# Chunk attention and SoLU feed-forward on one core: one copy for the turned probabilities of tiles 0 to 5, v loaded by halves of heads

## The chip, the cores and the metric

The kernel runs on one core of a Trainium2 chip. The metric is the device time of one execution in microseconds (us), taken as the median of several runs. Engines are named as in the profile: PE (TensorE matmul), PEld (its weight loads), DVE (VectorE), ACT (ScalarE), POOL (GpSimd) and SP (SyncE, which here only issues transfers; SPq is its queue).

## The reference

Attention inside chunks of 64 tokens, then a feed-forward layer on the joined heads:

```
B, H, S, D = 8, 8, 576, 64                  # 9 chunks of 64 tokens per batch
scores = q_c @ k_c^T / sqrt(D)               # within each chunk
attn   = softmax(scores)
x      = (attn @ v_c), heads joined          # 4608 tokens x 512
h      = x @ w_in                            # 512 -> 1024
e      = exp(h - max(h));  sm = e / sum(e)
solu   = h * sm
ln     = (solu - mean) / sqrt(var + 1e-6) * g_ln
out    = ln @ w_out                          # 1024 -> 512
```

## The kernel before

The 4608 tokens are cut into 36 tiles of 128 tokens, each of two chunks (c = 0, 1) of 64. The eight heads are taken as four pairs (hp), with j = 0, 1 inside a pair. Matrix products of the feed-forward layer are made of three products of rounded parts (`wi_l`, `wi_h`, `wo_l`, `wo_h` are the low and high parts of the weights).

The program has two parts. The first tiles and the preparation of the weights are an order written out by hand, the string START: each word is a step with its arguments, and the words are run one after the other; each engine does its instructions in the order in which they were issued. The words that matter here: `P:x` loads a raw unit of weights (0 to 3 for w_in, 4 to 7 for w_out), `n:i` loads q and k of tile i in their natural layout into the tile `nat` (two slots, used in turn), `v:i` loads v of tile i (`load_v`), `N:i:x` turns q or k on PE, `S:i` makes the scores (`scores`), `A:i` and `B:i` the softmax, `T:i` turns the probabilities of tiles 0 to 5 on PE and copies them out (`attn_transpose`), `V:i` makes the product with v (`values`, then `x_high` on ACT and `x_low` on DVE), `b`, `c`, `C`, `t`, `d` prepare a unit of weights (w_b, w_a, their join, high part, low part), `M:i` is the first feed-forward product, `w` is a matmul without a use that fills time. `K` and the loop behind START do the rest of the tiles, with PE as the engine that the order is built around.

Every transfer of START goes out on SP's queue, one behind the other. The framework gives the transfers eight landing counters (DMAHW0 to DMAHW7) in turn, so each one's issue waits until the transfer eight places before it has landed.

Probabilities. `scores` puts tile i's scores into `sx`, with the chunk's 64 query tokens on partitions c * 64 and the pair member j choosing one of two banks. Softmax gives `s_e`, 128 tokens x 8 heads x 64 keys. `attn_transpose` turns it with four PE transposes into a bank `tp`, so that partition j * 64 + key and column hp, query token hold a probability. The product with v needs, on chunk c's 64 partitions of `attn_t` (AT), the keys of chunk c for all heads, since v's tokens of chunk c lie on those partitions. So four ACT copies (c by j) take 64 partitions each, half of them from one half of the partitions to the other. Tiles from 6 on are turned by DVE and moved by transfers instead (`attn_turn`).

Of the kernel before, what the change touches and what calls it, by code (L numbers as in the profile page):

```python
# [65 lines left out]
def chunk_attention_then_solu_ffn(  # L66
# [15 lines left out]
    CH = 64  # L82
    NCH = S // CH
    HP = H // 2
# [7 lines left out]

    MS = nc.gpsimd
    PE_TURNED = 6
    PH2 = (1,)
    ORD = 5

# [12 lines left out]
    def po():  # L110
# [10 lines left out]
    pe, dve, act, pool, sync = (  # L121
        order.engine(e)
        for e in (nc.tensor, nc.vector, nc.scalar, nc.gpsimd, nc.sync)
    )
# [3 lines left out]
    def queue_of(word):  # L128
        return {"pool": pool, "act": act}.get(moved.get(word), sync)
# [7 lines left out]
    def bank():  # L137
        return ps_t.tile([P, FF // 2], F32, name="tp")
# [120 lines left out]
    QT, KT, V, QS, KS = {}, {}, {}, {}, {}  # L259
# [17 lines left out]
    AT = const.tile([P, 2, 2, H, 32], F32, name="attn_t")  # L277
# [23 lines left out]
    def chunk_of(i, c):  # L301
        n = 2 * i + c
        return n // NCH, n % NCH
# [19 lines left out]
    def tile_parts(i):  # L323

        (b0, n0), (b1, n1) = chunk_of(i, 0), chunk_of(i, 1)
        if b0 == b1:
            return [(0, P, b0, n0 * CH)]
        return [(0, CH, b0, n0 * CH), (CH, P, b1, n1 * CH)]
# [9 lines left out]

    def load_v(i):
        V[i] = work.tile([P, H, D], F32, name="v_sb", bufs=4)  # L340
        for p0, p1, b, s in tile_parts(i):
            arriving[i // 2].insert(0, queue_of(f"v:{i}").dma_start(
                V[i][p0:p1], v[b, :, s:s + p1 - p0, :].rearrange("h t d -> t h d")
            ))
# [19 lines left out]
    sx = ps_a.tile([P, 2, 2, HP, CH], F32, name="sx")  # L364
    sy = None

    def attn(i):
        return sy if order.on and i % 2 else sx

    def scores(i):  # L370
        sx = attn(i)
        for hp in range(HP):
            for c in range(2):
                for j in range(2):
                    rows, cols = slice(j * D, (j + 1) * D), slice(c * CH, (c + 1) * CH)
                    pe.matmul(
                        sx[cols, j, 0, hp],
                        QT[i][rows, hp, cols],
                        KT[i][rows, hp, cols],
                        start=True,  # L380
                        stop=True,
                    )
# [24 lines left out]
    def softmax_b(i):  # L407
# [6 lines left out]
        yield  # L414
        a = st[i, "e"] = work.tile([P, H, CH], F32, name="s_e") if i < PE_TURNED else e
        (pool if f"B:{i}" in moved else dve).tensor_tensor(
# [3 lines left out]
    def attn_transpose(i):  # L420

        a = st.pop((i, "e"))
        pt = bank().rearrange("p (a t) -> p a t", t=P)
        for hp in range(HP):
            pe.transpose(
                pt[:, hp, :],
                a[:, 2 * hp:2 * hp + 2, :].rearrange("p j k -> p (j k)"),
                ident,
            )
        yield  # L430
        for c in range(2):
            cols = slice(c * CH, (c + 1) * CH)
            to = AT[cols, :, i % 2].rearrange("p g (h j) t -> p j h g t", j=2)
            for j in range(2):
                act.copy(
                    to[:, j],
                    pt[j * CH:(j + 1) * CH, :, cols].rearrange(
                        "p h (g t) -> p h g t", t=32
                    ),
                )  # L440

    def attn_turn(i):
        a = st.pop((i, "e"))
# [17 lines left out]
    def values(i):  # L463
        sx = attn(i)
        for hp in range(HP):
            for j in range(2):
                for c in range(2):
                    rows = slice(c * CH, (c + 1) * CH)
                    pe.matmul(
                        sx[j * D:(j + 1) * D, c, 1, hp],  # L470
                        V[i][rows, 2 * hp + j, :],
                        AT[rows, :, i % 2, 2 * hp + j, :],
                        start=True,
                        stop=True,
                    )

    def start_values(i):
        values(i)
        yield
        x_high(i)  # L480
        yield
        x_low(i)
# [19 lines left out]
    def ffn_in(i):  # L502
        xh, xl = st[i, "x"]
        pool_h = ps_h2 if i in PH2 else ps_h
        ph = st[i, "h"] = pool_h.tile([P, 2, HALF], F32, name="ph")
# [254 lines left out]
    def warm(n):  # L760
# [9 lines left out]
    todo = {  # L770
        "P": load_pair, "n": load_natural,
        "v": load_v, "g": load_g, "Q": load_batch, "q": load_some,
        "G": scale_g, "N": turn_natural, "S": scores, "A": start_softmax, "B": softmax_b,
        "T": attn_transpose, "U": attn_turn, "V": start_values, "c": unit_scale,
        "b": unit_bits, "C": unit_join, "t": unit_high, "d": unit_low, "M": ffn_in, "X": solu_a, "Y": solu_b,
        "R": variance, "Z": z_turn, "z": z_half, "F": product, "o": store, "O": store_one,
# [18 lines left out]
    for i in range(first, NT):  # L795
# [7 lines left out]
        if i + 3 < NT:  # L803
            load_v(i + 3)
# [12 lines left out]
        if odd:  # L817
            for m in (i + 1, i + 2):
                if m + 2 < NT:
                    scores(m + 2)  # L820
                if m < NT:
                    values(m)
# [78 lines left out]
```

## Time and profile before

| | |
|---|---|
| median of 3 runs | 473.31 us (472.98 to 473.34) |
| the profiled execution | 471.33 us, of it 469.5 us span |
| PE busy | 461.0 us (98%) |
| PEld, DVE, ACT, POOL busy | 381.4, 368.4, 260.7, 149.3 us |
| granted clock of PE | 0.999 of full speed |
| DMA busy, first 24.37 us / rest | 0.99 / 0.66 |

The span runs from the first to the last instruction. An engine's busy share is an average over the whole span; where an engine is always busy, what counts is when it gets its first work and what makes it wait.

### The profile page before, as it was taken

The page shows a single profiled execution, that of the slowest core. Times are in us where ns is not written, and L with a number is a line of the kernel's source. Part 1 is how long each engine was busy: PE and PEld are TensorE (multiplying, and loading weights), DVE is VectorE, ACT ScalarE, POOL GpSimd, SP SyncE. Part 2 cuts the span into 40 slices and gives each one's busy share as a digit, 9 for nine tenths or more (in the row PEclk, how much of TensorE's full clock was granted, in tenths as well). Part 3 has the DMA queues.
Part 4 walks back from the last instruction along what each step waited for, and adds up shares of the span by engine and source line. Part 5 has one row for each costly group of instructions (what it writes and reads, how often), then busy time and mean ns, then how long its engine had stood idle before and what let it go on. Part 6 is the DMA issues. An engine that isn't in the chain of part 4 may idle for free.

```text
span 469.5 us, 11066 instructions
## 1 busy us (share of the span) xinstructions
PE 461.0 (98%) x4210; PEld 381.4 (81%) x4210; DVE 368.4 (78%) x516; ACT 260.7 (56%) x425; POOL 149.3 (32%) x300
## 2 busy tenths in 40 slices
PE   8799999999999999999999999999999999999997
PEld 6588887888888888888888888888888888888886
DVE  1999997988779887878788878787979797954441
ACT  4889985554544555454646464545545454545451
POOL 1116536150505151505050505042505141424430
PEclk9999999999999999999999999999999999999999
DMA  9999989778886788786267696858644434343221
GB/s 253 305 285 244 194 145 179 163 194 144 200 147 173 136 202 143 186 153 178 52 162 142 162 163 171 160 138 170 157 108 111 114 99 128 87 116 100 72 77 66
DMA packets 192924, 72.57 MB, mean 155 GB/s; under 512 B 177188, under 2 KB 177960, under 8 KB 191976
## 3 DMA queue, kind: packets, MB, share of 16 engines
q1 hardware_dynamic: 186200, 58.89, 56.1%
q0 software_dynamic: 6528, 12.86, 10.4%
q8 instruction: 33, 0.54, 0.5%
q14 instruction: 19, 0.16, 0.1%
q10 hardware_dynamic: 144, 0.13, 0.1%
HBM read 36.70 MB, written 9.44 MB: 98 GB/s over the span
## 4 chain that ended last, share of the span: by engine, by line
PE 93%; DMA 2%; ACT 2%; SPq 2%; DVE 1%; issue 0%; DVEq 0%; ACTq 0%
PE po L57 42%; PE ph L57 41%; PE tp L57 6%; PE sx L57 5%; DMA w_raw<-in_moe_w_in_dram 2%; SPq L57 2%; DVE z_b L57 1%; ACT attn_t L57 0%; ACT wi_h L57 0%; ACT z L57 0%; ACT w_a L57 0%; ACT z_h L57 0%; ACT w_b L57 0%; ACT o_sb L57 0%; ACT kT L57 0%
## 5 line engine op out<-in xcount | busy, mean ns | idle before, releaser
L57 ACT ACTIVATE z<-ph,h_nmax 128x1024 f32<-128x1024 f32 x36 | 40.2, 1116 | 131.7 <-DVE h_nmax L57 131.6
L57 PE MATMUL po<-wo_l,z_h 128*128 128x512 f32 (+1 forms) x288 | 113.1, 393 | 0.0
L57 PE MATMUL ph<-wi_l,x_h 128*128 128x512 f32 x288 | 112.9, 392 | 0.0
L57 PE MATMUL ph<-wi_h,x_h 128*128 128x512 f32 x288 | 112.1, 389 | 0.0
L57 PE MATMUL po<-wo_h,z_l 128*128 128x512 f32 (+1 forms) x288 | 111.6, 387 | 0.0
L57 PE MATMUL po<-wo_h,z_h 128*128 128x512 f32 (+1 forms) x288 | 111.5, 387 | 0.0
L57 POOL DMA_DIRECT2D z_t<-z_b x144 | 71.8, 506 | 23.7 <-DVE z_b L57 19.7
L57 PE MATMUL ph<-wi_h,x_l 128*128 128x512 f32 x288 | 77.7, 389 | 0.0
L57 POOL TENSOR_TENSOR u<-ssq,eps 128x1 f32<-128x1 f32 x36 | 7.2, 199 | 219.2 <-ACT sq L57 219.1
L57 DVE TENSOR_REDUCE h_nmax<-ph 128x1 f32<-128x1024 f32 x36 | 44.0, 1222 | 32.0 <-PE ph L57 32.0
L57 PEld LDWEIGHTS po<-wo_l,z_h 128*128 128x128 f32 x288 | 54.1, 188 | 11.4
L57 PEld LDWEIGHTS ph<-wi_h,x_l 128*128 128x128 f32 x288 | 54.1, 188 | 11.4
L57 PEld LDWEIGHTS po<-wo_h,z_l 128*128 128x128 f32 x288 | 54.1, 188 | 11.1
L57 PEld LDWEIGHTS ph<-wi_h,x_h 128*128 128x128 f32 x288 | 54.1, 188 | 10.9
L57 PEld LDWEIGHTS ph<-wi_l,x_h 128*128 128x128 f32 x288 | 54.1, 188 | 10.9
L57 PEld LDWEIGHTS po<-wo_h,z_h 128*128 128x128 f32 x288 | 54.1, 188 | 10.4
L57 DVE TENSOR_TENSOR z_l<-z_t,z_h 128x1024 fp32r<-128x1024 f32 (+1 forms) x37 | 42.0, 1136 | 21.2 <-ACT z_h L57 20.0
L57 DVE SCALAR_TENSOR_TENSOR z<-ph,z 128x1024 f32<-128x1024 f32 x36 | 44.0, 1223 | 13.3 <-ACT z L57 13.3
L57 ACT ACTIVATE z<-z,z_sum 128x1024 f32<-128x1024 f32 x33 | 38.1, 1154 | 23.7 <-DVE z L57 22.7
L57 DVE STREAM_TRANSPOSE z_b<-z 128x1024 f32<-128x1024 f32 x34 | 41.2, 1212 | 6.8 <-ACT z L57 3.9
L57 ACT CAST z_h<-z_t 128x1024 fp32r<-128x1024 f32 (+1 forms) x37 | 35.9, 971 | 8.5 <-PE po L57 3.9
L57 ACT ACTIVATE o_sb<-po,r 128x512 f32<-128x512 f32 (+1 forms) x36 | 24.3, 674 | 27.2 <-POOL r L57 20.9
(79 smaller groups left out, 592.9 us busy)
## 6 DMA issues: line engine op xcount, KB each, us to landing
out_dram<-o_sb SPq DMA_DIRECT2D x35, 256.0 KB, 2.4
v_sb<-in_v_dram SPq DMA_DIRECT2D x32, 256.0 KB, 4.5
z_t<-z_b POOLq DMA_DIRECT2D x128, 64.0 KB, 2.7
z_t<-z_b SPq DMA_DIRECT2D x128, 64.0 KB, 2.9
q_st<-in_q_dram SPq DMA_DIRECT2D x96, 72.0 KB, 3.0
k_st<-in_k_dram SPq DMA_DIRECT2D x96, 72.0 KB, 3.0
w_raw<-in_moe_w_out_dram SPq DMA_DIRECT2D x4, 1024.0 KB, 7.1
attn_t<-a_b POOLq DMA_DIRECT2D x60, 64.0 KB, 3.7
```

The costliest lines, as they stand in the source:

```text
L57: ins = make(*args, **kwargs)
```

## The change

For tiles 0 to 5 the turned probabilities stay on the partitions on which the turn leaves them. One ACT copy of 128 partitions x 512 elements takes the place of four of 64 x 256. For that, v of these tiles is loaded so that the half of the partitions says which member of a pair it is, and the column says chunk and pair: four transfers of 64 partitions x 4 heads in place of one of 128 x 8 (or of two of 64 x 8 for tile 4, which spans two batches). In the second chunk the two heads of a pair change places; so each group of four small products in a row (64 rows x 64 columns of the array each) still meets all four quarters of the array, in another order. `scores` does the exchange by writing to the other bank for tiles 0 to 7, and `values` reads accordingly; tiles 6 and 7 keep their way of loading v and of turning.

```
+    SWAPPED = 8
...
     def load_v(i):
         V[i] = work.tile([P, H, D], F32, name="v_sb", bufs=4)
+        if i < PE_TURNED:
+            heads = v.rearrange("b (a j) t d -> b j a t d", j=2)
+            for c in range(2):
+                b, n = chunk_of(i, c)
+                for half in range(2):
+                    queue_of(f"v:{i}").dma_start(
+                        V[i][half * CH:(half + 1) * CH, c * HP:(c + 1) * HP],
+                        heads[b, half ^ c, :, n * CH:(n + 1) * CH, :].rearrange("a t d -> t a d"),
+                    )
+            return
...
     def scores(i):
-                        sx[cols, j, 0, hp],
+                        sx[cols, j ^ c if i < SWAPPED else j, 0, hp],
...
     def attn_transpose(i):
-        for c in range(2):
-            cols = slice(c * CH, (c + 1) * CH)
-            to = AT[cols, :, i % 2].rearrange("p g (h j) t -> p j h g t", j=2)
-            for j in range(2):
-                act.copy(
-                    to[:, j],
-                    pt[j * CH:(j + 1) * CH, :, cols].rearrange(
-                        "p h (g t) -> p h g t", t=32
-                    ),
-                )
+        act.copy(
+            AT[:, :, i % 2].rearrange("p g h t -> p h g t"),
+            pt.rearrange("p h (c g t) -> p (h c) g t", c=2, t=32),
+        )
...
     def values(i):
-                    rows = slice(c * CH, (c + 1) * CH)
+                    half, of, at = c, 2 * hp + j, 2 * hp + (j ^ c if i < SWAPPED else j)
+                    if i < PE_TURNED:
+                        half, of, at = j ^ c, c * HP + hp, 2 * hp + c
+                    rows = slice(half * CH, (half + 1) * CH)
                     pe.matmul(
                         sx[j * D:(j + 1) * D, c, 1, hp],
-                        V[i][rows, 2 * hp + j, :],
-                        AT[rows, :, i % 2, 2 * hp + j, :],
+                        V[i][rows, of, :],
+                        AT[rows, :, i % 2, at, :],
```

What that makes of the order of the instructions, at three places. First SP's queue at tile 0's v, before:

```order
L57 DMA v_sb<-in_v_dram 128x8x64 [waits DMAHW0_49]
L57 DMA w_raw<-in_moe_w_in_dram 128x2048 [waits DMAHW1_49]
L57 DMA nat<-in_q_dram 128x8x64 [waits DMAHW2_49,PE_49]
L57 DMA nat<-in_k_dram 128x8x64 [waits DMAHW3_49,PE_49]
L57 DMA w_raw<-in_moe_w_in_dram 128x2048 [waits DMAHW4_49]
L57 DMA nat<-in_q_dram 128x8x64 [waits DMAHW5_49,PE_49]
```

The rows are v of tile 0, weight unit 2, q and k of tile 2, weight unit 3 and q of tile 3. The same place now:

```order
L57 DMA v_sb<-in_v_dram 64x4x64 [waits DMAHW0_49]
L57 DMA v_sb<-in_v_dram 64x4x64 [waits DMAHW1_49]
L57 DMA v_sb<-in_v_dram 64x4x64 [waits DMAHW2_49]
L57 DMA v_sb<-in_v_dram 64x4x64 [waits DMAHW3_49]
L57 DMA w_raw<-in_moe_w_in_dram 128x2048 [waits DMAHW4_49]
L57 DMA nat<-in_q_dram 128x8x64 [waits DMAHW5_49,PE_49]
L57 DMA nat<-in_k_dram 128x8x64 [waits DMAHW6_49,PE_49]
L57 DMA w_raw<-in_moe_w_in_dram 128x2048 [waits DMAHW7_49]
L57 DMA nat<-in_q_dram 128x8x64 [waits DMAHW0_49,PE_49]
```

Three more issues stand ahead of the weight units 2 and 3 and of q and k of tiles 2 and 3, and unit 3 now waits for the landing of unit 1, eight places before it. Tiles 1, 2, 3 and 5 get three more issues each in the same way, tile 4 two: 17 in all.

Second, ACT at tile 0's copies, before:

```order
L57 ACTIVATE w_a<-w_a 128x1024 [waits DVE_49,Activation_49]
L57 COPY attn_t<-tp 64x4x2x32 [waits PE_49]
L57 COPY attn_t<-tp 64x4x2x32 x3
L57 CAST wi_h<-w_a 128x1024 [waits DVE_49]
L57 COPY kT<-tp 128x512 [waits PE_49]
L57 CAST x_h<-sx 128x512 [waits PE_49]
```

And now:

```order
L57 ACTIVATE w_a<-w_a 128x1024 [waits DVE_49,Activation_49]
L57 COPY attn_t<-tp 128x8x2x32 [waits PE_49]
L57 CAST wi_h<-w_a 128x1024 [waits DVE_49]
L57 COPY kT<-tp 128x512 [waits PE_49]
L57 CAST x_h<-sx 128x512 [waits PE_49]
```

Nothing else on ACT moves; the other five places read the same way.

Third, PE from the turn of tile 2's k to the scores of tile 2, before:

```order
L57 MATMUL tp<-ident,nat 128x128 [waits DMAHW3_49,PE_49,Activation_49]
L57 MATMUL tp<-ident,nat 128x128 x3
L57 MATMUL sx<-attn_t,v_sb 64x64 [waits DMAHW0_49]
L57 MATMUL sx<-attn_t,v_sb 64x64 x15
L57 MATMUL sx<-kT,qT 64x64 [waits DVE_49,Activation_49]
```

And now:

```order
L57 MATMUL tp<-ident,nat 128x128 [waits DMAHW6_49,Activation_49]
L57 MATMUL tp<-ident,nat 128x128 x3
L57 MATMUL sx<-attn_t,v_sb 64x64 [waits DMAHW0_49]
L57 MATMUL sx<-attn_t,v_sb 64x64 [waits DMAHW3_49]
L57 MATMUL sx<-attn_t,v_sb 64x64 [waits DMAHW1_49]
L57 MATMUL sx<-attn_t,v_sb 64x64 [waits DMAHW2_49]
L57 MATMUL sx<-attn_t,v_sb 64x64 x12
L57 MATMUL sx<-kT,qT 64x64 [waits DVE_49,Activation_49]
```

The 16 products of `values` stand where they stood, and the first four each wait for one of v's four transfers.

## Rows read from the trace of the kernel before

**Rows 1.** Windows: length, PE, PEld, DVE, ACT, POOL busy us, clock, DMA, GB/s.

```profile
0.00:24.37 24.37, 19.54 (x202) 15.28 (x203) 13.55 (x20) 16.60 (x22) 4.18 (x13) 1.00 0.99 274
24.37:469.50 445.13, 441.43 (x4008) 366.17 (x4008) 354.85 (x497) 244.11 (x404) 145.15 (x288) 1.00 0.66 148
```

**Rows 2.** PE's waits from 0 to 90 us: total us, times, longest.

```profile
PE tp L57 <- DVE e L57: 0.4, 1, 0.4
```

**Rows 3.** Timeline of PE: start, length, operation, in brackets idle time before it.

```profile
19.71 0.63 PE L57 MATMUL tp<-ident,nat 128*128 128x128 f32 x4 [0.99 <-DMA nat<-in_q_dram]
20.71 0.64 PE L57 MATMUL tp<-ident,nat 128*128 128x128 f32 x4 [0.37 <-ACT attn_t L57]
21.29 0.69 PE L57 MATMUL sx<-attn_t,v_sb 64*64 64x64 f32 x32
22.98 0.69 PE L57 MATMUL sx<-kT,qT 64*64 64x64 f32 x32 [1.00 <-ACT x_h L57]
...
24.37 0.63 PE L57 MATMUL tp<-ident,nat 128*128 128x128 f32 x4
...
30.48 0.65 PE L57 MATMUL sx<-attn_t,v_sb 64*64 64x64 f32 x32
```

**Rows 4.** Transfers issued at 4.64, 10.08 and 16.87 us: size, us to landing.

```profile
w_raw<-in_moe_w_in_dram SPq DMA_DIRECT2D x1, 1024.0 KB, 8.7
...
nat<-in_k_dram SPq DMA_DIRECT2D x1, 256.0 KB, 10.5
...
nat<-in_q_dram SPq DMA_DIRECT2D x1, 256.0 KB, 7.4
```

**Rows 5.** Timeline of ACT.

```profile
19.15 1.49 ACT L57 COPY attn_t<-tp 64x256 f32<-64x256 f32 x4
20.67 1.16 ACT L57 CAST wi_h<-w_a 128x1024 fp32r<-128x1024 f32 x1
21.85 0.59 ACT L57 COPY kT<-tp 128x512 f32<-128x512 f32 x1
```

**Rows 6.** Timeline of DVE.

```profile
19.28 1.23 DVE L57 SCALAR_TENSOR_TENSOR w_a<-w_a,w_b 128x1024 uint32<-128x1024 uint32 x1 [0.29 <-ACT w_a L57]
```

**Rows 7.** Timeline of SP's queue: start and length of the issue.

```profile
8.30 0.43 SPq L57 DMA_DIRECT2D v_sb<-in_v_dram  x1
...
10.08 3.13 SPq L57 DMA_DIRECT2D nat<-in_k_dram  x1
13.26 3.52 SPq L57 DMA_DIRECT2D w_raw<-in_moe_w_in_dram  x1
16.87 1.63 SPq L57 DMA_DIRECT2D nat<-in_q_dram  x1
```

**Rows 8.** v of tiles 1, 5, 4, issued at 25.06, 45.28, 46.95 us: size, us to landing.

```profile
v_sb<-in_v_dram SPq DMA_DIRECT2D x1, 256.0 KB, 4.9
...
v_sb<-in_v_dram SPq DMA_DIRECT2D x1, 256.0 KB, 8.0
...
v_sb<-in_v_dram SPq DMA_DIRECT2D x1, 128.0 KB, 6.9
```

**Rows 9.** Products with v: 30 ns (PE, PEld busy, instructions, clock, DMA, GB/s); durations in ns.

```profile
21.28:21.31 0.03, 0.02 (x4) 0.03 (x4) 1.00 0.94 213
...
L57 PE MATMUL sx<-attn_t,v_sb x288: 218/218/267, 21.3 to 133.8; 64*64 64x64 f32 x144
```

**Rows 10.** SP's queue at v of tile 3 and behind v of tile 4.

```profile
40.52 3.74 SPq L57 DMA_DIRECT2D v_sb<-in_v_dram  x1
...
48.60 2.40 SPq L57 DMA_DIRECT2D q_st<-in_q_dram  x1
```

**Rows 11.** Chain that ended last: start, length, what.

```profile
84.54 1.39 PE sx L57 x61
...
108.90 1.09 PE sx L57 x64
```

**Rows 12.** Transfer issued at 82.92 us, the last for tiles 6 and 7's probabilities.

```profile
attn_t<-a_b SPq DMA_DIRECT2D x1, 64.0 KB, 2.2
```

## The prediction

> **What bounds the kernel now.** I read the busy windows first, then PE's waits, its timeline before the last large gap, and for each gap what it waited for. From 24.37 us to the end PE is busy for 441.4 of 445.1 us [rows 1] (the rest is mostly the ends of small products that the profile models). In the list of waits only one lies behind that point, 0.4 us for DVE [rows 2]. So the kernel is 24 us of start and then PE work in a row. What the change is worth is decided by what lets PE begin at 24.37, by whether something new makes it wait later, and by whether its products take longer.
>
> In the start the transfers are the limit: DMA is busy 0.99 of the time at 274 GB/s [rows 1]. PE's two turns for tile 2 wait, the first for q's landing, the second, by the profile, for ACT's copies of the probabilities [rows 3]. But k of tile 2, which that turn reads, landed at 10.08 + 10.5 = 20.58 us [rows 4], 0.13 before it started. The turn at 24.37 reads q of tile 3, landed at 16.87 + 7.4 = 24.27 [rows 4]. PE is in the hands of the loads at both places.
>
> **ACT: four copies become one.** Four took 1.49 us [rows 5]. The new operation is not in the trace; the nearest row is ACT's copy of 128 x 512 out of the same kind of bank, 0.59 [rows 5], and with its pieces of 32 elements it could take up to what two of the old ones take, 0.75. I take 0.59: 0.90 saved per tile, 5.4 us of ACT time over six tiles. Of these only tile 0's copy stands before 24.37. It would end at 19.74 instead of 20.64. Behind it on ACT stands the high part of a weight unit, which needs a DVE join ending at 19.28 + 1.23 = 20.51 [rows 6]; it starts at about 20.53 instead of 20.67, and k's copy, x_h and the scores of tile 2 (which waited for x_h, [rows 3]) come 0.14 earlier. The turn of tile 2's k gains at most 0.1, to its landing. All of that ends at the turn of tile 3's q, which cannot start before 24.27: the gain is 0 to 0.1 us. The cover is that landing; without it the gain would be 0.14 by the join, and never more than the 0.90 saved. The five later copies lie beside a PE that does not wait: 0. The one later gap (0.4) waits for DVE [rows 2], not for a copy.
>
> **SP: 17 more issues.** One issue of v takes 0.43 us when nothing holds it, and some 0.05 lies between two [rows 7]. Three more for tile 0 are 3 x 0.48 = 1.44 us, ahead of weight unit 2, q and k of tile 2, unit 3 and q of tile 3. The cover is the issue at 10.08: it took 3.13 us where the same kind takes 0.43, so the queue stood for 2.7 us because it was full, as it did in the two issues behind it [rows 7]. The three issues go into that standing time, and unit 3 goes out at about 13.3 as before. Its new wait, for the landing of unit 1 at 4.64 + 8.7 = 13.34 [rows 4], costs 0.1 there, taken up by its own 3.5 us of standing. I take 0 at q of tile 3. The bounds are 0 and +1.44, all issues in the open. For tile 1 the same cover holds only if data ahead of v is still under way: v landed at 25.06 + 4.9 = 29.96 [rows 8] and its products began at 30.48 [rows 3], 0.52 of slack against 1.44, so 0 with an upper bound of +0.9. For tiles 3, 5 and 4 there are 3 + 3 + 2 issues, 3.8 us, against 3.3 us of standing in tile 3's issue (3.74 less 0.43) and 2.0 in the first q_st behind tile 4's (2.40 less 0.43) [rows 10]: 0, if nothing of it is left over.
>
> **The transfers.** Bytes and pieces of 256 bytes are the same. The nearest row for smaller transfers is tile 4's v, already in halves: 45.28 + 8.0 = 53.28 for the transfer ahead, 46.95 + 6.9 = 53.85 for the first half [rows 8], so 128 KB in 0.57 and 256 KB in 1.14, where 274 GB/s gives 0.96. At worst 0.2 us per tile, 0 if it is only rounding; I take 0.05 for what reaches q of tile 3. The Trainium skill speaks against this edit: "DMA: Bandwidth & Descriptors", section "Rules for kernel authors", says that two transfers to disjoint halves of the partitions serialize and should be one, and its section "Bandwidth" puts a 64 KB transfer at 0.95 us; by that, as an estimate, tile 0's v would take 3.8 us, and the sum would end near 476. The trace has transfers of half the size following each other in 0.57, which disagrees with that price.
>
> **PE's products.** The 16 products of `values` (32 records) take 0.69 us [rows 3]. In the first 30 ns four are under way, each recorded at 218 ns or more [rows 9]: all four quarters of the array at once, two of them fed by the same half of the rows. The new order meets the same quarters once per four, with neighbours in the same half of the rows; I take 0. The new waits on v's pieces (18 in all) are for transfers that landed before: 0. The first is covered best, since tile 0's v was issued at 8.30 and is used at 21.29.
>
> **The one place without slack later.** At 84.54 the products of tile 6 take 1.39 us for 61 records, where 64 take 1.09 at 108.90 [rows 11]: they wait for probabilities whose last transfer landed at 82.92 + 2.2 = 85.12 [rows 12]. SP's queue sets when that goes out, so whatever is left over of the extra issues would be paid here in full. The last piece of tile 4's v now has the landing of weight unit 7 eight places ahead of it, a wait that can leave something over; I take 0.1. The bounds are -0.3 (1.39 down to 1.09, that wait gone) and +2.4 (five issues of tiles 5 and 4 in the open).
>
> **Sum.** -0.05 (ACT) + 0.05 (transfers) + 0 (SP in front) + 0 (PE) + 0.1 (place at 85) = +0.1 us on the profiled execution: 471.33 to 471.4. The median of the runs lies 2.0 above it, so 473.31 + 0.1 = **473.4 us**.
>
> **Rivals.**
> A. SP's issues show in front. For: the queue is the only one for all loads, and a full queue is my reading of long issues, not a row. Against: 2.7 us of cover for 1.44. It decides once less than 1.44 is covered. +1.4: 474.7, slower.
> B. They show at 85 us: extra issues that are not absorbed by the full queue near 48 us push the transfers for tile 6. For: no slack there. Against: 5.3 us of standing for 3.8. +2.4: 475.7.
> C. Neighbours in the same half of the rows can't overlap, and the six bursts of `values` take twice their 0.6: +3.5, 476.8. Against: [rows 9]. The Trainium skill, "TensorE: Matmul & The Clock Gate", section "The mechanism" of Part 3, says that a weight load overlaps running matmuls only where the row group differs, which would make for this rival; the trace, with four under way in 30 ns, does not agree.
> D. The relief of ACT comes through: if q of tile 3 is not what holds the turn at 24.37, the front gains up to 0.9, and with the wait at 85 us gone (-0.3) and the 0.4 gap closed up to 1.6: 472.4 to 471.7, faster. Against: landing and start are 0.1 apart.
>
> **How the numbers follow.** Forecast (within 0.9 us of 473.3, which is 0.2%, about what a measurement of this kernel can tell from no change) 0.75; A 0.08, B 0.05, C 0.03, D 0.09. Slower: 0.16, all of A, B and C. Faster: 0.08, D but for its near end. Same: 0.76, the forecast and that end. The range leaves out C, most of B and the far end of D: 472.4 to 474.8. The forecast's own range is 472.7 to 474.0.
>
> **What would show it.** In the changed profile: one copy near 0.6 us at 19.1, and ACT's busy time near 255; the issues at 8.3 take some 2 us together and the one of tile 2's k stands shorter by as much; q of tile 3 lands at 24.2 to 24.4 and PE has no gap behind it but the two known ones; bursts of `values` stay at 0.69. The prediction is wrong if that landing moves by 0.5 or more in either direction, if a burst lengthens, or if the products at 85 us wait longer.

## The result and the profile after

The changed kernel takes 477.72 us (median of 7 runs, 475.17 to 479.43). Beside it the kernel before takes 473.31 (7 runs, 471.88 to 473.99): a ratio of 1.0096, 95% interval 1.0067 to 1.0125, so 4.4 us slower. The profiled execution took 477.72, its span 475.9 us, 6.4 more than the span before. That is more than the medians differ by, because the profiled execution of the kernel before, 471.33 us, lies below the median of its kernel.

From the page of the changed kernel, the busy times and the shares of the chain that ended last:

```profile
PE 461.5 (97%) x4210; PEld 381.4 (80%) x4210; DVE 371.0 (78%) x516; ACT 255.3 (54%) x407; POOL 148.4 (31%) x300
...
PE 82%; SPq 9%; DMA 7%; issue 1%; ACT 1%; DVE 1%; DVEq 0%; ACTq 0%
```

PE is busy for as long as before (461.5 us against 461.0). ACT has 5.4 us less. SP's queue (9%) and transfers (7%) hold 16% of the chain, where they held 4%. The copy itself, in ACT's timeline:

```profile
19.59 0.58 ACT L57 COPY attn_t<-tp 128x512 f32<-128x512 f32 x1
```

PE's timeline answers to [rows 3] and [rows 11]. In brackets stands the idle time before a row:

```profile
21.18 0.69 PE L57 MATMUL sx<-attn_t,v_sb 64*64 64x64 f32 x32
...
24.32 0.63 PE L57 MATMUL tp<-ident,nat 128*128 128x128 f32 x4
...
30.88 0.69 PE L57 MATMUL sx<-attn_t,v_sb 64*64 64x64 f32 x30 [0.19 <-DMA v_sb<-in_v_dram]
39.87 0.63 PE L57 MATMUL tp<-ident,nat 128*128 128x128 f32 x4 [0.54 <-DMA nat<-in_k_dram]
52.90 0.63 PE L57 MATMUL sx<-attn_t,v_sb 64*64 64x64 f32 x27 [1.25 <-DMA v_sb<-in_v_dram]
76.52 0.63 PE L57 MATMUL tp<-ident,nat 128*128 128x128 f32 x4 [2.43 <-DMA nat<-in_k_dram]
91.00 0.30 PE L57 MATMUL sx<-attn_t,v_sb 64*64 64x64 f32 x2 [0.99 <-DMA attn_t<-a_b]
91.72 0.63 PE L57 MATMUL sx<-attn_t,v_sb 64*64 64x64 f32 x27 [0.42 <-DMA attn_t<-a_b]
```

The start is as before: the turn of tile 3's q stands at 24.32 (24.37 before), and a burst of products with v still takes 0.69. Behind it PE, which had waited once for 0.4 us, waits six times, for 5.8 us together, always for a transfer that SP issues: v of tiles 1 and 3, k of tiles 5 and 8, the probabilities of tile 6. In the chain a row that stood at 86.91 before (24 products `po`) stands at 93.34: by then the whole difference of the spans, 6.4 us, is there.

SP's queue, issue by issue, answers to [rows 7] and [rows 10]:

```profile
8.17 2.73 SPq L57 DMA_DIRECT2D v_sb<-in_v_dram  x4
...
12.14 1.08 SPq L57 DMA_DIRECT2D nat<-in_k_dram  x1
...
25.04 4.04 SPq L57 DMA_DIRECT2D v_sb<-in_v_dram  x4
...
27.02 2.05 SPq L57 DMA_DIRECT2D v_sb<-in_v_dram  x1
...
29.12 1.08 SPq L57 DMA_DIRECT2D w_raw<-in_moe_w_out_dram  x2
...
32.88 6.03 SPq L57 DMA_DIRECT2D v_sb<-in_v_dram  x4
...
41.22 0.78 SPq L57 DMA_DIRECT2D w_raw<-in_moe_w_out_dram  x1
...
43.27 7.80 SPq L57 DMA_DIRECT2D v_sb<-in_v_dram  x4
...
51.75 5.52 SPq L57 DMA_DIRECT2D v_sb<-in_v_dram  x8
57.38 2.70 SPq L57 DMA_DIRECT2D q_st<-in_q_dram  x5
...
71.43 0.44 SPq L57 DMA_DIRECT2D nat<-in_q_dram  x1
...
78.99 7.22 SPq L57 DMA_DIRECT2D z_t<-z_b  x8
...
87.67 2.44 SPq L57 DMA_DIRECT2D attn_t<-a_b  x4
```

The row at 27.02 is the last of the four pieces counted in the row at 25.04. The same queue in the kernel before, at places that were not shown:

```profile
46.95 0.61 SPq L57 DMA_DIRECT2D v_sb<-in_v_dram  x1
...
65.62 0.43 SPq L57 DMA_DIRECT2D nat<-in_q_dram  x1
...
73.13 6.38 SPq L57 DMA_DIRECT2D z_t<-z_b  x8
...
81.07 2.45 SPq L57 DMA_DIRECT2D attn_t<-a_b  x4
```

In front the cover held in this execution: the four issues of tile 0 take 2.73 us, and k of tile 2 stands 1.08 where it stood 3.13. From tile 1 on SP falls behind. Against before it is 8.8 us late at the first q_st (57.38 against 48.60), 5.8 at q of tile 8 (71.43 against 65.62), 5.9 at z_t and 6.6 at the probabilities of tile 6. PE follows with 6.4. A quarter of v (one of its four pieces) takes 2.73 / 4 = 0.68 us of the queue with its gap.

What the engines of the transfers did meanwhile, from the windows (PE, PEld, DVE, ACT and POOL busy, granted clock, DMA share, GB/s), first the kernel before, then the changed one:

```profile
25.00:50.00 25.00, 25.00 (x280) 20.60 (x279) 23.05 (x34) 22.65 (x43) 11.28 (x8) 1.00 1.03 280
```

```profile
25.00:30.00 5.00, 5.00 (x30) 3.99 (x32) 4.96 (x8) 3.87 (x6) 0.00 (x0) 1.00 0.53 113
28.00:30.00 2.00, 2.00 (x15) 1.53 (x17) 1.97 (x5) 1.26 (x2) 0.00 (x0) 1.00 0.15 30
...
25.00:50.00 25.00, 24.27 (x271) 19.67 (x270) 22.74 (x33) 19.88 (x33) 6.86 (x6) 1.00 0.85 228
```

Before, the DMA engines are full from 25 to 50 us. Now they are half empty in the first five of these, while SP issues pieces of 64 KB, and by 50 us 25 x (280 - 228) = 1300 KB fewer have moved, some 4.6 us of their work at 280 GB/s. Not all of that is issue time: the piece issued at 27.02 holds SP for 2.05 us, where the others take 0.61 to 0.63, and meanwhile the engines run nearly dry (0.15 from 28 to 30 us). What that issue waits for, no view shows.

### The profile page after: what moved, and what is told of

Same layout as the page of the kernel before. It is cut to its first block, busy times and chain, and to the rows that moved or that the text cites. A ratio compares the mean times of both kernels' runs of the same rounds, so it can differ in the third digit from the quotient of the medians.

```text
span 475.9 us, 11061 instructions
## 1 busy us (share of the span) xinstructions
PE 461.5 (97%) x4210; PEld 381.4 (80%) x4210; DVE 371.0 (78%) x516; ACT 255.3 (54%) x407; POOL 148.4 (31%) x300
## 4 chain that ended last, share of the span: by engine, by line
PE 82%; SPq 9%; DMA 7%; issue 1%; ACT 1%; DVE 1%; DVEq 0%; ACTq 0%
PE po L57 39%; PE ph L57 35%; SPq L57 9%; PE sx L57 4%; PE tp L57 4%; DMA nat<-in_k_dram 3%; DMA w_raw<-in_moe_w_in_dram 1%; DMA w_raw<-in_moe_w_out_dram 1%; DMA v_sb<-in_v_dram 1%; DMA attn_t<-a_b 0%; DVE w_a L57 0%; ACT wi_h L57 0%; ACT x_h L57 0%; ACT w_a L57 0%; ACT w_b L57 0%
## 5 line engine op out<-in xcount | busy, mean ns | idle before, releaser
L57 ACT ACTIVATE o_sb<-po,r 128x512 f32<-128x512 f32 (+1 forms) x36 | 24.2, 673 | 28.9 <-POOL r L57 20.9
```

The costliest lines, as they stand in the source:

```text
L57: ins = make(*args, **kwargs)
```

## The experiments

The theories: 1, the time of SP's issues, which stand in one queue ahead of all that follows; 2, the pieces themselves (64 partitions, small transfers). The third theory is the new order of the products in the first runs and the number of transfers in the later ones; each expectation says it. An estimate goes with the runs: the time that the issues of v, or what stands in their place, add to SP's queue, from the issue times with their gaps in the traces (a quarter 0.66, a piece of two heads 0.51, a tiny transfer 0.46, a whole v 0.48, a half 0.65 us).

**v of tiles 1 to 5 issued by POOL.** Edit: to the table of moved steps of the changed kernel

```
+ v:1=pool v:2=pool v:3=pool v:4=pool v:5=pool
```

> The changed kernel with the v pieces of tiles 1 to 5 issued by POOL in place of SP (tile 0's stay on SP); the transfers keep their shape. Theory 1 (what costs is the place on SP's queue: 14 more issues of some 0.65 us each and the window of eight landings make k of tiles 5 and 8, v of tile 3 and the probabilities of tiles 6 and 7 late): k of tile 8 goes out near 66 us again, PE's waits for loads behind 30 us go from about 6 us to under 2, and the time is 473 to 474. Theory 2 (the pieces of 64 partitions and 4 heads move slower through the DMA engines, whoever issues them): the waits stay, 476 to 478. Theory 3 (the small products take longer in the new order): 476 to 478, with longer bursts.

Measured: 475.67 (474.62 to 476.26), ratio 1.005 (1.0029 to 1.0072). That lies between the numbers of theories 1 and 2. About half of the loss is gone. But the front is worse: PE waits 2.2 us at 27.83 for q of tile 3, which lands at 27.7 (24.2 in the changed kernel) and is under way together with v of tile 1 from POOL. So SP's time counts; how much, this run can't say.

**The copy, the exchange and the order of products alone.** Edit in the changed kernel's `load_v`, so that v is loaded whole and lies where the new products don't expect it:

```
-        if i < PE_TURNED:
+        if False:
```

> The changed kernel with v of all tiles loaded whole as before, so that v of tiles 0 to 5 lies in the wrong places and the output is not the reference's; the one copy, the exchange in the scores and the new order of the products stay. Theories 1 and 2: 472.5 to 473.7, like the kernel before, ACT near 255 us busy. Theory 3 (products or banks): 475 or more.

Measured: 473.25 (470.98 to 474.3), ratio 0.9994 (0.9966 to 1.0023). ACT's relief of 5.4 us brings nothing and the new order of products costs nothing. In its trace no wait of PE lies behind 24 us (PE is late there by itself: its granted clock of 0.91 is taken up below), and from 25 to 50 us the DMA engines are full again:

```profile
25.00:50.00 25.00, 25.00 (x271) 20.76 (x270) 21.38 (x31) 18.36 (x31) 8.55 (x6) 0.91 1.01 272
```

**The quarters alone.** Edit in the kernel before: v of tiles 0 to 5 in four transfers of 64 partitions x 4 heads, to where it lay before.

```
+        if i < PE_TURNED:
+            for c in range(2):
+                b, n = chunk_of(i, c)
+                for half in range(2):
+                    queue_of(f"v:{i}").dma_start(
+                        V[i][c * CH:(c + 1) * CH, half * HP:(half + 1) * HP],
+                        v[b, half * HP:(half + 1) * HP, n * CH:(n + 1) * CH, :].rearrange("a t d -> t a d"),
+                    )
+            return
```

> The kernel before with v of tiles 0 to 5 in four transfers of 64 partitions x 4 heads, data in the old places, nothing else changed. Theories 1 and 2: the whole loss, 476 to 479, with the waits for k of tile 8 and v of tile 3 as in the changed kernel. Theory 3: 473 to 474.

Measured: 479.23 (477.05 to 479.45), ratio 1.0122 (1.0078 to 1.0165). Together with the run before it that shows that the whole loss lies in the way v is loaded. (12.1 us of issues added.)

**17 tiny transfers.** Edit in the kernel before, ahead of each whole v:

```
+    spare, spares = const.tile([16, 17, 8], F32, name="spare"), []
-    const.tile([P, 208], F32, name="pad")
...
+        if i < PE_TURNED:
+            for x in range(4 - len(tile_parts(i))):
+                sync.dma_start(spare[:, len(spares)], g_ln.rearrange("(a p) -> a p", p=64)[:, :8])
+                spares.append(i)
```

> The kernel before with 17 more issues on SP, ahead of v of tiles 0 to 5, of 16 partitions x 8 numbers into memory that nothing reads (a small unused spacer in memory is left out for it); v whole as before. Theory 1: an issue costs SP nearly the same whatever it moves, and it takes one of eight landing counters: 475 to 478, k of tile 8 issued 4 us or more later than before's 66.6. Theory 2: 473 to 474, since there are no bytes of the slow kind.

Measured: 474.68 (472.65 to 476.2), ratio 1.0026 (1.0001 to 1.005). That is below theory 1's 475 to 478 and above theory 2's 473 to 474. The same number of extra issues costs a quarter of the loss; but they are shorter, 7.8 us in all.

**Four pieces of all 128 partitions.** Edit in the kernel before:

```
+        if i < PE_TURNED:
+            parts = tile_parts(i)
+            n = 2 * len(parts)
+            for p0, p1, b, s in parts:
+                for h in range(0, H, n):
+                    queue_of(f"v:{i}").dma_start(V[i][p0:p1, h:h + n], ...)
+            return
```

> The kernel before, with v of tiles 0 to 5 in four transfers each, but of two heads on all 128 partitions (tile 4, which spans two batches: four heads on 64 partitions); the data lie where they lay before. As many transfers as in the changed kernel (24 in place of 7), another shape. Theory 1 (SP's time): what costs is the time that SP spends on issues, in which nothing else is sent; if such an issue takes about the 0.42 us of a tiny one, 24 of them take some 8 us more than the seven of before, near the 17 tiny ones, and the time is 474.3 to 475.5 us; if it takes 0.61 us as the quarters do, 478.5 to 480. Theory 2 (the shape): transfers to 64 partitions move slower; with all partitions back the loss is gone but for tile 4, 473 to 474.5, whatever an issue takes. Theory 3 (the count): eight landing counters are used up four times as fast; 478 to 480, whatever an issue takes.

Measured: 474.87 (473.02 to 479.78), ratio 1.005 (1.0019 to 1.0082). Its row of SP's queue at tile 1:

```profile
25.11 2.16 SPq L57 DMA_DIRECT2D v_sb<-in_v_dram  x4
```

2.16 / 4 = 0.54 us where the quarters take 0.68: 9.1 us added by the estimate, near the tiny ones in time as in loss. The count of transfers is that of the quarters, so by the median the count alone (theory 3) does not make the loss. But the runs spread widely, and the profiled one is the slowest. In it PE waits longer for k of tile 8 than in any run with quarters:

```profile
77.66 1.09 PE L57 MATMUL tp<-ident,nat 128*128 128x128 f32 x4 [3.78 <-DMA nat<-in_k_dram]
```

**29 tiny transfers,** six issues in place of each whole v (the edit as above, `range(6 - ...)`).

> The kernel before, v whole, with 29 tiny transfers (16 x 6 elements of g_ln to a tile without a use) put on SP's queue ahead of v of tiles 0 to 5: six issues in place of each whole v. 29 issues at about 0.46 us with their gap are 13.3 us of SP's time, about what the quarters added (24 at 0.66 less 7 at about 0.46 are 12.6). The unused pad tile is left out for their room. Theory 1 (SP's time): the loss is that of the quarters, 477.5 to 480, and the DMA engines' share in 25 to 30 us falls to some 0.6. Theory 2 (the shape of the pieces): v is unchanged, so no more than the 17 tiny ones, 474 to 475.5. Theory 3 (the count): more transfers than ever, 479 to 482.

Measured: 483.03 (480.69 to 484.57), ratio 1.0215 (1.0166 to 1.0263). More than theory 1 expected (477.5 to 480) and more than theory 3 did (479 to 482), which is the nearer; against theory 2, since v is whole. So it speaks for SP, but not for the time of the issues alone: their number may count too. SP's queue and PE's waits in its trace:

```profile
24.80 2.46 SPq L57 DMA_DIRECT2D spare<-in_moe_g_ln_dram  x5
27.30 1.54 SPq L57 DMA_DIRECT2D v_sb<-in_v_dram  x1
```

```profile
PE tp L57 <- DMA nat<-in_k_dram: 4.0, 1, 4.0
PE sx L57 <- DMA v_sb<-in_v_dram: 2.6, 3, 1.5
```

Transfers that move nothing to speak of, in front of an unchanged v, make the same two waits as the quarters. They cost about twice what the quarters do, with nearly the same issue time. In the profiled execution, the lowest of the four, PE waits for 7.1 us behind 24 us, 1.3 more than in the changed kernel, and behind the longest wait its clock falls (below). That all of v stands behind the extra issues here, where a quarter's data go out with each, may be why the waits are longer; no run shows it.

**Tiles 0 to 2 alone, tiles 3 to 5 alone, tile 0 alone.** Edit: the quarters of above under `if i < 3`, `if 3 <= i < PE_TURNED`, `if i < 1`.

> The kernel before, with v in quarters for tiles 0, 1 and 2 alone, data in their old places. Theory 1 (SP's time, DMA engines dry in 25 to 30 us): tile 0's issues stay hidden in the front; those of tiles 1 and 2 (some 4.4 us of SP) make all that follows late, 474.8 to 476.5, about half of the loss of all six tiles. A rival place, that only what stands right ahead of the second preparation's transfers and of q and k of tile 8 counts: 473 to 474.

> The kernel before, with v in quarters for tiles 3, 4 and 5 alone, data in their old places. Theory 1: SP's 6 us more between 40 and 57 us make q and k of tile 8 late by 3 to 5 us, 475 to 477. If the two halves' losses add up, this and the run with tiles 0 to 2 together make the 5.9 us of all six tiles; if a wait absorbs what was lost before it, they make more than that.

> The kernel before, with v in quarters for tile 0 alone (data in their old places): three issues more, 2.2 us of SP, between 8 and 11 us, where the front hides them. By the prediction and by theory 1 no change: 472.8 to 474.

Measured: tiles 0 to 2, 475.04 (473.74 to 477.75), ratio 1.0046 (1.002 to 1.0073); tiles 3 to 5, 475.77 (472.83 to 478.18), ratio 1.0054 (1.0026 to 1.0081); tile 0, 474.07 (471.99 to 475.44), ratio 1.0025 (1.0003 to 1.0048). The two halves make 1.0100 together, so the loss is spread over the tiles. Tile 0 is not quite free, as I had expected: its ratio is just beyond the bound. Over the profiled executions q of tile 3 lands at 24.2 to 24.8 us where v of tile 0 is whole (six kernels with nothing else changed in front, mean 24.4), and at 24.2 to 25.7 where it is in quarters (eight, mean 25.0).

**Late v on POOL; q and k of tile 8 on POOL; both; and two controls.** Edits in the table of moved steps, of the changed kernel three times, of the kernel before twice:

```
+ v:3=pool v:4=pool v:5=pool
+ n:8=pool
+ v:3=pool v:4=pool v:5=pool n:8=pool
```

> The changed kernel, with the quarters of v of tiles 3, 4 and 5 issued by POOL, those of tiles 0, 1 and 2 still by SP. Pieces, count and data as in the changed kernel; SP now has 12 issues of v fewer than that, and 4 fewer than before the change after 40 us. Theory 1 (SP's time is what is lost): most of what tiles 3 to 5 cost comes back and the loss of tiles 1 and 2 stays, 473.5 to 475.5; q and k of tile 8 are issued by 68 us. If the pieces themselves were what costs (their shape or count), 477 or more. If POOL's queue holds up s_e and the raw parts of the weights behind the twelve issues, 476 to 478, with waits of PE on POOL's s_e.

> The changed kernel, with q and k of tile 8 issued by POOL and not by SP, where they stand behind 32 transfers of the second preparation. Theory 1: their issue no longer hangs on SP, the waits of PE for them (2.4 us each way in the changed kernel's profile) go, and what v of tiles 2 and 3 lost by 53 us (2.85 us) stays: 474.5 to 476.5. A rival, that the DMA engines are full there and another wait comes in their place (attn_t of tile 6, z_t): 477 to 478.5.

> The changed kernel, with both: v of tiles 3, 4 and 5 and q and k of tile 8 issued by POOL. Theory 1: only tiles 1 and 2 still load SP beyond the kernel before, 472.5 to 475. If a wait of another kind stands behind, 475 or more.

> A control: the kernel before, with q and k of tile 8 issued by POOL. In its profile PE waits 0.4 us for q of tile 8, so 472.5 to 473.5; if it gains more than 1 us, moving this pair is a gain of its own, and the run with it on the changed kernel has to be read against this one.

> A control to the run with late v on POOL: the kernel before, v whole, with the four transfers of v of tiles 3, 4 and 5 issued by POOL. If POOL's queue has a price of its own (its s_e and weight parts behind the issues, unit 7 beside its transfers), 474.5 to 476.5, and that run's missing gain is explained by it; if it is free, 472.5 to 474, and the pieces cost on any queue.

Measured: late v, 476.28 (475.7 to 476.87), ratio 1.0091 (1.0065 to 1.0118); q and k of tile 8, 479.11 (475.93 to 480.54), ratio 1.0133 (1.008 to 1.0185); both, 476.63 (476.01 to 478.08), ratio 1.0103 (1.0073 to 1.0133). The controls: 471.75, ratio 0.9998 (0.9974 to 1.0022) with q and k of tile 8 moved, and 472.27, ratio 0.9992 (0.9968 to 1.0016) with late v moved whole; both a little below what was expected and no different from the kernel before. All three on the changed kernel miss theory 1's numbers. With q and k of tile 8 moved, PE's timeline shows why:

```profile
91.39 0.29 PE L57 MATMUL sx<-attn_t,v_sb 64*64 64x64 f32 x2 [3.30 <-DMA attn_t<-a_b]
```

No wait stands at 76 us any more, and the time comes back at 91, since SP issues the probabilities of tile 6 just as late (at 88.4 us, 87.7 in the changed kernel). One wait less does not make the queue earlier. With late v moved, POOL's issues in the changed kernel and in the control, below each the row of PE that waits for the weights:

```profile
40.58 5.18 POOL L57 DMA_DIRECT2D v_sb<-in_v_dram  x8
...
51.74 2.50 POOL L57 DMA_DIRECT2D v_sb<-in_v_dram  x4
...
64.65 0.50 PE L57 MATMUL po<-wo_l,z_h 128*128 128x512 f32 x1 [0.77 <-DVE wo_l L57]
```

```profile
39.96 2.05 POOL L57 DMA_DIRECT2D v_sb<-in_v_dram  x2
...
49.20 1.42 POOL L57 DMA_DIRECT2D v_sb<-in_v_dram  x2
...
63.75 0.50 PE L57 MATMUL po<-wo_l,z_h 128*128 128x512 f32 x1 [0.76 <-DVE wo_l L57]
```

The quarters take 7.7 us of POOL, the whole ones 3.5, and POOL's last part of the weights comes 2.5 us later (57.50 against 54.99). That PE pays for it is not shown: it waits for the weights behind it equally long in both. The spans of the two profiled executions differ by 1.9 us (473.8 and 471.9). That lies in the front, where v of tile 0 is still in quarters (scores of tile 2 at 24.41 and 23.43), and in the waits for the probabilities of tile 6 (1.8 us and 1.0). The medians differ by 4.0, and the rest of that stays open.

**Half of the issues of the second preparation taken away,** from the changed kernel and from the kernel before. Edit in `qk_loads` (and `q:8` becomes `q:4`):

```
+            if b == 2:
+                p0 = (h % 2) * D
+                sync.dma_start(t[p0:p0 + D, h // 2].rearrange("p g t -> p (g t)"),
+                               src[b, h].rearrange("(p r) d -> p (r d)", r=NCH))
+                return
...
-        return loads
+        return loads[::2] if b == 2 else loads
```

> The changed kernel, with q_st and k_st of batch 2 loaded by 16 transfers of 64 partitions x 576 contiguous elements in place of 32 of 32 x 18 x 32: the same bytes, but put in wrong places, so that tiles 9 and on compute with wrong q and k. SP has 16 issues of some 0.54 us fewer, 8.6 us, between 57 and 78 us. Theory 1 (SP's queue is one string of issues without slack, what is lost before 57 us is carried on to q and k of tile 8 and to attn_t): both waits go, and what v lost by 53 us stays, 2 to 2.9 us: 475 to 476.5. Theory 2 (the pieces themselves, or what they do to the DMA engines): 477 or more, with the waits for tile 8 or attn_t still there.

> The control to the run before it: the kernel before, with the same 16 transfers in place of 32 (data of batch 2 in wrong places). PE waits only 0.5 us between 24.3 and 93 us there, so a relief of SP has little to give: 472.3 to 473.6 by either theory.

Measured: changed kernel 473.1 (471.46 to 475.24), ratio 1.0017 (0.9998 to 1.0036); kernel before 471.64 (470.15 to 474.94), a little below what was expected, ratio 0.9984 (0.9956 to 1.0011). The distance between the two kernels shrinks from 0.96% to 0.33%, of which some 1.6 us are left, with all 24 quarters still there. SP's queue in the changed kernel so relieved, and all waits of PE that its view lists:

```profile
57.42 5.02 SPq L57 DMA_DIRECT2D q_st<-in_q_dram  x8
...
66.02 0.53 SPq L57 DMA_DIRECT2D nat<-in_q_dram  x1
...
82.05 2.44 SPq L57 DMA_DIRECT2D attn_t<-a_b  x4
```

```profile
PE tp L57 <- DMA nat<-in_q_dram: 1.6, 2, 1.3
PE ph L57 <- POOL e L406: 1.4, 1, 1.4
PE sx L57 <- ACT x_h L57: 1.3, 1, 1.3
PE tp L57 <- ACT attn_t L57: 1.1, 1, 1.1
PE tp L57 <- DVE s_e L57: 0.9, 1, 0.9
PE sx L57 <- ACT kT L57: 0.7, 1, 0.7
```

SP is as late as ever at 57.42, but back at the place of before (65.62, 81.07) for q of tile 8 and nearly so for the probabilities. No wait for v_sb, k of tile 8 or attn_t by transfer is left, and PE's last idle time lies at 24.96 us. That is theory 1: what PE pays is SP's lateness. The time fell further than it expected. In the profiled execution the wait for v of tile 3 is gone too, since PE was later there (scores of tile 2 at 24.96, 23.16 in the changed kernel, and then a lower clock) and v came as before. The relief itself is enough for the other two: k of tile 8 and the probabilities go out more than 5 us earlier, and PE had waited 2.4 and 1.4 for them.

**PE's granted clock in these traces.** In the profiled executions of the kernel before and of the changed kernel the granted clock is 1.00 (2.4 GHz) all through these 100 us. In others it falls to 0.50 (1.2 GHz) for a stretch. Three of these stretches, in this order: four pieces of 128 partitions, behind the wait of 3.78 us; 29 tiny transfers, behind the wait of 3.95; the changed kernel with half of the issues, behind the gaps in front.

```profile
77.00:83.00 6.00, 5.34 (x44) 4.15 (x44) 2.82 (x5) 0.20 (x2) 1.93 (x5) 0.50 1.30 183
79.00:82.00 3.00, 3.00 (x10) 2.51 (x9) 2.20 (x3) 0.00 (x0) 0.85 (x3) 0.50 1.31 189
23.00:29.00 6.00, 4.66 (x67) 4.14 (x61) 4.96 (x7) 4.97 (x7) 1.14 (x1) 0.50 1.15 195
```

The same stands behind the wait of 3.30 us with q and k of tile 8 on POOL (0.50 from 93 to 96 us) and behind 2.81 us with the quarters alone. At 0.50 a product of 128 x 512 takes 0.63 us where it takes 0.39 at 1.00, so a long wait costs more than its length: as an estimate some 1.7 us more with the tiny transfers (half of a stretch of 3.4 us), and some 3 with the four pieces. The theories leave that out. In front, between 20 and 32 us, the clock falls in nine of the eighteen profiled executions, the control with q and k of tile 8 moved among them, so the pieces are not needed for it. PE is then late by itself, and a late transfer no longer makes it wait: the traces of v of tiles 1 to 5 on POOL, of the copy alone, of the 17 tiny transfers and of the changed kernel with half of the issues are of that kind, and that they show no later wait is in part due to it. The ratios are of all executions and do not hang on one trace.

## Why the prediction was wrong

The runs beside the estimate of issue time added, in order of it:

| v of tiles 0 to 5 | issues added, us | ratio |
|---|---|---|
| quarters, tile 0 | 2.2 | 1.0025 |
| quarters, tiles 3 to 5 | 5.7 | 1.0054 |
| quarters, tiles 0 to 2 | 6.5 | 1.0046 |
| 17 tiny ahead | 7.8 | 1.0026 |
| four pieces of 128 partitions | 9.1 | 1.0050 |
| quarters, all (alone; the change) | 12.1 | 1.0122; 1.0096 |
| 29 tiny ahead | 13.3 | 1.0215 |

Up to 9 us a sixth to a half of the issue time shows, at 12 to 13 us a third to three quarters. Shape and count don't order the runs; SP's time does, but only roughly: the intervals of the middle rows overlap, and waits, clock and lateness of PE in front differ from execution to execution.

**The front.** That it is bounded by loads and that the four issues go into the standing time of the queue: right in the profiled execution (24.32, and the issue of k of tile 2 shorter by 2.05). But the reason given for the cover, a full queue, was mostly not the right one. SP's waits in the kernel before, from 9 to 11 us, say what 1.9 of the 2.7 us were; the line below it, from 40 to 100 us, is the wait of the first q_st, issued at 48.60:

```profile
SPq L57 <- PE tp L57: 1.9, 1, 1.9
...
SPq L57 <- POOL r L57: 2.2, 1, 2.2
```

So the cover in front was a wait for PE to be done with the slot of `nat`. Over many executions q of tile 3 is some 0.6 us later, so rival A (less covered than needed, up to 1.4 us lost) holds for a part of its price.

**ACT.** 0.59 for the copy: 0.58. ACT at 255: 255.3. Worth 0: the copy alone has the ratio 0.9994. Rival D did not come.

**PE's products.** 0.69 and no new cost: right, rival C did not come.

**The step that failed** is the sum for the later tiles: "For tiles 3, 5 and 4 there are 3 + 3 + 2 issues, 3.8 us, against 3.3 us of standing in tile 3's issue [...] and 2.0 in the first q_st [...]: 0, if nothing of it is left over", and with it the 0.1 at 85 us. Three things were wrong in it. The price: an issue of 64 partitions takes 0.66 to 0.68 with its gap, not 0.48, although it moves a quarter of the bytes of the row that I took it from. The trace before had the nearer row, half of tile 4's v at 46.95: 0.61, 0.65 with its gap. The list: tile 2's three issues are in no sum, and tile 1's were weighed only against tile 1's own products, not against the weight units behind them. And the cover: I took every standing issue for a reserve of time. Two are different. The standing issue of tile 3 ends shortly before the weight unit three places ahead (`P:7`) has landed, in the kernel before (40.52 + 3.74 = 44.26; the unit at 37.53 + 6.9 = 44.4) as after (first of four pieces 43.27 + 5.38 = 48.65; the unit at 41.22 + 7.7 = 48.9). So its end goes with data ahead, and these data were late by then: the unit went out 3.7 us later, behind a stretch in which SP issued pieces and the DMA engines stood half empty (113 GB/s from 25 to 30 us). This standing was no reserve. That of the first q_st was one: it ended when POOL was done with its buffer (the 2.2 us above), and 1.9 of its 2.40 us are gone in the changed kernel, where five issues take 2.70. That a standing queue means busy engines does not hold either: the issue at 27.02 stands while they run dry. The 0.1 hung on the wait of tile 4's last piece for a weight unit (called 7 there; by START it is `P:6`); that wait came, with 0.3 us, and is not the loss.

**Rival B** named the right place and the right direction, at 475.7 with a chance of 0.05. Its price, five issues in the open (2.4 us), was too small: SP was 6.6 us late there. In the stretch from the first q_st to q of tile 8 it gave back 3.0 us (17.0 us before, 14.05 after), of which 1.9 is the first q_st's.

**What had spoken against it.** The Trainium skill, "DMA: Bandwidth & Descriptors", section "Rules for kernel authors", spoke against two transfers to disjoint halves, and the direction was right. Its reason did not show: pieces on all partitions cost too, and 24 pieces of 64 KB cost less once other issues made room (0.33% in place of 0.96%). The Trainium skill, "Perfetto Trace Analysis", section "What 'DMA-bound' means", has the case that did occur, an issuing engine whose track is solid with issues; the trace agrees, SP from 51 to 78 us. Its section "DMA Optimizations" says that spreading issues over engines may then help; here, with POOL, it gave half back in one run and nothing in another.

**Open.** Why late v on POOL gives nothing back in the median, what holds the issue at 27.02, and how much of SP's lateness is the time of the issues and how much the number of transfers. With 17 more transfers the loss grows with the time (7.8, 9.1 and 12.1 us: 1.0026, 1.0050 and 1.0122), though the shape changes too; at nearly the same time, 12.1 and 13.3 us, it grows with the number (17 and 29 more: 1.0122 and 1.0215). Both may count. That 29 tiny transfers cost twice the quarters is explained in part, by longer waits and the clock behind them. No version was found that beats the kernel before: PE waits there for 0.4 us behind 24.37, so a shorter queue has nothing to win.

## What to carry to other kernels

Splitting a transfer costs issue time on the queue that sends it, times the pieces, and everything behind it in that queue is late by what is not absorbed; price it by an issue of the very shape, since half the partitions can take longer than the whole. A long issue on a queue is not always a reserve to be filled with further issues: ask what it waits for. If it ends when another engine is done with a buffer, the time is there; if data ahead in the same queue have to land, the new issues make that late as well. Where the queue is one string to the next place that has no slack, sum the issues from the change to that place, and look for its last consumer rather than for the first wait, because removing one wait moves the loss to the next. And look at the granted clock before reading waits from a trace: a long wait can be followed by a stretch at half the clock, and a PE that is late by itself hides late transfers.

## What the runs showed of the hardware

An issue of SP that nothing holds takes 0.43 us for v whole (128 partitions x 8 heads), 0.47 for 128 x 2, 0.61 for 64 x 4 and 0.42 for 16 x 8 single elements: 128 x 2 and 64 x 4 are the same bytes in as many pieces, so the spread over partitions counts. Behind a unit of 1 MB transfers of 64 KB land some 0.3 us apart (tile 5's quarters, issued from 51.75 every 0.65 us, take 5.4, 5.1, 4.8 and 4.5 us), so one issued every 0.66 us can't keep the engines full. A transfer of 1 MB takes longer beside those of another queue: the weight unit `P:6`, issued 2 to 3 us earlier than before, took 14.4 us to land beside quarters from POOL and 13.3 beside whole v from POOL, where it took 6.7 with all loads on SP's queue. And behind waits of PE of 2.8 to 4.0 us the granted clock stood at 0.50 for a stretch in five executions.
